# An hourglass-attention and dense kernel rewritten: four-token rows, plane order, key tiles every 112 tokens, PSUM seats given by the plan

## The chip, the cores and the metric

The kernel runs on one core of a Trainium2 chip. The metric is device time in microseconds (us), the median of several executions. A core has TensorE (PE, with its weight loads as PEld), VectorE (DVE), ScalarE (ACT) and GpSimd (POOL); SyncE (SP) issues most transfers, and 16 DMA engines move the data. Matmul results land in PSUM, which has eight banks of 512 float32 columns on 128 partitions; everything else on the chip lies in SBUF.

## The reference

Attention over 8 batches of 8 heads, 576 tokens, 64 features, and then a two-layer dense block on its result:

```python
# q, k, v: (8, 8, 576, 64); factor = 4
q_d, k_d, v_d = means over groups of 4 tokens          # 144 pooled tokens
out_d = softmax(scale * q_d @ k_d.T) @ v_d              # pooled attention
out_up = np.repeat(out_d, 4, axis=2)
mask = np.abs(pos[:, None] - pos[None, :]) < 4          # a band of 7 keys
out_local = softmax(where(mask, scale * q @ k.T, -1e9)) @ v
x = (out_up + out_local), as 4608 tokens x 512
h = x @ w_in                                            # 512 -> 2048
return (h - np.tanh(h)) @ w_out                         # 2048 -> 512, float32
```

## The kernel before

**Work units.** Attention goes by pairs of heads: 32 pairs p, four to a batch. The dense block goes by nine blocks kb of 512 tokens; each has 16 column tiles of `mm1` (four matmuls of 512 columns each, L609) and 16 parts of `mm2` (four each, L636), so there are 1152 dense matmuls. All matmuls are in bf16.

**Order.** Nothing is scheduled by the framework. `Program.op` records each operation with its engine, an estimated duration, keys that it reads and writes, and a priority; `choice` records one that may go to several engines. `order()` is a list scheduler: it plays the engines forward, gives each the ready operation with the lowest priority number, and `emit` writes all instructions in that order of start times. Each engine executes its own in order. Attention has priority 10p, dense matmuls 5000, so dense work fills what attention leaves on PE. Where the plan shows PE idle before the first dense block, `emit` puts filler matmuls (L773).

**One pair.** q and k are loaded as rows of nine tokens (`load_qk`, L291), v as five windows of 128 tokens, one every 120 tokens (`load_v`, L310 to L316). The casts of L408 give `qr`. In the first 16 pairs PE transposes `qr` in nine matmuls (L433) and ACT puts the result in token order in `qk` (L437); from pair 16 on a DMA transpose does it, with two ACT copies (L424). L449 and L454 add four tokens to one for pooled q and k (`half`, `qkd`). Local scores (L468) are ten matmuls of 64 rows, one for each head and query tile of 120 (the last of 96); pooled scores (L484) are four of 144 columns. The two heads use rows 0 to 63 and 64 to 127, and their matmuls run at the same time. ACT takes exponentials (L501, L511, L514), DVE multiplies by the band mask (L504, L517). The outputs (`outs`) are 18 matmuls of 65 columns, nine for each head: five for the local tiles (L528) and four for two blocks of pooled queries (L535), each over two parts of the pooled keys. The 65th column of v gives the sums; L544 takes reciprocals, L546 scales seven blocks into `ln`.

Pooled v comes from PE for pairs below 16 (`pool_v`, six matmuls of 256 columns for two pairs, L381 and L383, in parts of 128 rows), later from a load of four-token rows and two POOL additions (L364, L368), in two parts of 72 rows.

**Back.** In pairs below 16 PE transposes `ln` back: one full matmul (L556), one of 16 rows (L557), five for the local tiles (L560); L587 and L589 add pooled and local result into `xT`. From pair 16 on a DMA transpose and L572, L578 do it.

**PSUM.** Fixed tiles: `ps_ts` and `ps_ox` for attention, two more of each kind for the first batch, whose four banks then become `ps_hy`, four slots that dense work uses in turn.

**Dense order.** Block 0 does all of `mm1` and all of `mm2`; block 1 does `mm1` alone; from block 2 on `mm1` of kb and `mm2` of kb - 1 alternate. The weights are loaded by POOL (L328, L332) as soon as certain v loads are issued.

Of the kernel before, what the change touches and what calls it, by code (L numbers as in the profile page):

```python
# [15 lines left out]
class Program:  # L16
# [6 lines left out]


    LAT = {"PE": 270, "ACT": 150, "DVE": 110, "POOL": 150, "SP": 50, "DMA": 1800}

    def __init__(self):
        self.ops = []
        self.alternatives = {}
        self.touch = []  # L30
        self.fresh = set()
        self.last_write = {}
        self.readers = {}

    def op(self, eng, ns, fn, reads=(), writes=(), pri=0):
        i = len(self.ops)
        deps = set()
        for key in reads:
            if key in self.last_write:
                deps.add(self.last_write[key])  # L40
        for key in writes:
            if key in self.last_write:
                deps.add(self.last_write[key])
            deps.update(self.readers.get(key, ()))
        for key in reads:
            self.readers.setdefault(key, set()).add(i)
        for key in writes:
            self.last_write[key] = i
            self.readers[key] = set()
        deps.discard(i)  # L50
        self.ops.append((eng, ns, fn, deps, pri))
        self.touch.append(set(reads) | set(writes))
        return i

    def choice(self, alternatives, reads=(), writes=(), pri=0):

        i = self.op(None, 0, None, reads, writes, pri)
        self.alternatives[i] = {a[0]: a for a in alternatives}
        return i

    def order(self):
        n = len(self.ops)
        users = [[] for _ in range(n)]
        left = [0] * n
        for i, (_, _, _, deps, _) in enumerate(self.ops):
            left[i] = len(deps)
            for d in deps:
                users[d].append(i)
        at = [0.0] * n
        free, ready, start = {}, {}, [None] * n  # L70

        def make_ready(i):
            for eng in self.alternatives.get(i, (self.ops[i][0],)):
                ready.setdefault(eng, []).append(i)
        for i in range(n):
            if left[i] == 0:
                make_ready(i)
        for _ in range(n):
            best = None
            for eng, cand in ready.items():  # L80
                if not cand:
                    continue
                now = max(free.get(eng, 0.0), min(at[i] for i in cand))
                if eng == "DMA":
                    pick = min((at[i], i) for i in cand)[1]
                else:
                    pick = min((self.ops[i][4], i) for i in cand if at[i] <= now)[1]
                if best is None or now < best[0]:
                    best = (now, eng, pick)
            now, eng, i = best  # L90
            if i in self.alternatives:
                for other in self.alternatives[i]:
                    ready[other].remove(i)
                self.ops[i] = self.alternatives[i][eng] + self.ops[i][3:]
            else:
                ready[eng].remove(i)
            start[i] = now
            end = now + self.ops[i][1]
            free[eng] = end
            for u in users[i]:  # L100
                same = self.ops[u][0] == eng and eng != "DMA"
                at[u] = max(at[u], end if same else end + self.LAT[eng])
# [3 lines left out]
        self.start, self.free = start, free  # L106
        return sorted(range(n), key=lambda i: (start[i], i))

    def idle(self, order, banks, until):

        pe = [i for i in order if self.ops[i][0] == "PE" and self.start[i] < until]
        found = []
        last = 600.0
        for i in pe:
            if self.start[i] - last > 350:
                for name, keys in banks.items():  # L120
                    prev = [e for s0, e, fresh in self.uses[name] if s0 < last]
                    after = [(s0, fresh) for s0, e, fresh in self.uses[name]
                             if s0 >= last]
                    if max(prev, default=0) <= last and (not after or after[0][1]):
                        room = min(self.start[i], after[0][0] if after else until) - last
                        found.append((i, name, room))
                        break
            last = self.start[i] + self.ops[i][1]
        return found

    def emit(self, banks=None, end=None, filler=None):
        order = self.order()
        fill = {}
        if filler:
            until = min(self.start[i] for i in range(len(self.ops)) if end in self.touch[i])
            self.uses = {name: sorted(
                (self.start[i], self.start[i] + self.ops[i][1] + 200, i in self.fresh)
                for i in range(len(self.ops)) if self.touch[i] & set(keys))
                for name, keys in banks.items()}
            for i, name, room in self.idle(order, banks, until):  # L140
                slow = 430 if self.start[i] < 6000 else 230
                fill[i] = (name, int(0.75 * room / slow))
        for i in order:
            if i in fill:
                filler(*fill[i])
            if self.ops[i][2] is not None:
                self.ops[i][2]()
# [3 lines left out]
def kernel(  # L151
# [15 lines left out]
    NHB = NPAIR // 2  # L167
    G = S // 4
    SCALE = 1.0 / float(D) ** 0.5
    A9 = 9  # L170
    G9 = S // A9
    QW = 120
    NT = 5
    NQ = [120, 120, 120, 120, 96]
    KOFF = 585
    N_FF = Dff // 128
    N_DC = Dm // 128
    NBLK = NTOK // 512

# [9 lines left out]
    NQKN, NVST, NVW = 4, 5, 3  # L189
# [3 lines left out]
    mask = fixed("mask", [128, 576], BF16)  # L193
# [3 lines left out]
    qkn = fixed("qkn", [128, 2, A9 * D], FP32, NQKN)  # L197
    vst = fixed("vst", [128, 2, NT, 64], FP32, NVST)
    vw = fixed("vw", [128, 4, NT, 65], BF16, NVW)
    vd = fixed("vd", [128, 2, 4, 65], BF16, NVW)  # L200
    qr = fixed("qr", [128, A9, 128], BF16, 2)
    qk = fixed("qk", [128, 1192], BF16, 2)
    qT = fixed("qT", [128, A9, 128], BF16, 2)
    half = fixed("half", [128, 2, G, 2], FP32)
    qkd = fixed("qkd", [128, 344], BF16, 2)
    v4 = fixed("v4", [72, 2, 2, 4 * D], FP32, 2)
    v2 = fixed("v2", [72, 2, 2, 2 * D], FP32)
    vp = fixed("vp", [72, 2, 2, D + 1], BF16, 2)
    E = fixed("E", [128, 1840], BF16, 2)
    lT = fixed("lT", [128, 7, 128], BF16, 2)  # L210
    warm = lT[0].rearrange("p n c -> p (n c)")[:, 0:512]
    r = fixed("r", [128, 2, 7], FP32, 2)
    ln = fixed("ln", [128, 7, 128], BF16, 2)
    od = fixed("od", [128, G], BF16, 2)
    gT = fixed("gT", [128, N_FF, 512], BF16, 2)
    u = fixed("u", [128, 512], FP32, 3)
    y = fixed("y", [128, Dm], FP32, 3)

    ps_ts = fixed("ps_ts", [128, 2, 512], FP32, pool=psum)
    ps_ox = fixed("ps_ox", [128, 2, 512], FP32, pool=psum)  # L220
    ps_hy = []


    early = ExitStack()
    psum_e = early.enter_context(tc.tile_pool(name="psum_e", bufs=1, space=PSUM))
    ps_ts1 = fixed("ps_ts1", [128, 2, 512], FP32, pool=psum_e)
    ps_ox1 = fixed("ps_ox1", [128, 2, 512], FP32, pool=psum_e)

    def dense_banks():
        early.close()  # L230
        pool = ctx.enter_context(tc.tile_pool(name="psum_d", bufs=1, space=PSUM))
        ps_hy.extend(fixed("ps_hy", [128, 512], FP32, 4, pool=pool))

    P = Program()
    op = P.op
    V, A, T, GP = nc.vector, nc.scalar, nc.tensor, nc.gpsimd


# [7 lines left out]

# [6 lines left out]
    def c_pick():  # L253

        V.memset(pick, 0.0)
        for t in range(4):
            V.tensor_copy(out=pick[:, t, 30 * t:30 * t + 30], in_=group[:, 1:31])
        V.tensor_copy(out=pick[:, 4, 120:128], in_=group[:, 1:9])
        V.tensor_copy(out=pick[:, 5, 112:128], in_=group[:, 9:25])

    def c_mask():

        GP.memset(mask, 1.0)
        m4 = mask[:, 0:480].rearrange("p (t c) -> p t c", c=QW)
        for part, pat in ((m4, [[0, 4], [1, QW]]),
                          (mask[:, 480:576], [[1, 96]])):
            neg = [[-s, n] for s, n in pat]
            GP.affine_select(
                out=part, in_=part, compare_op=ALU.is_ge, fill=0.0,
                base=-1, pattern=neg, channel_multiplier=1)  # L270
            GP.affine_select(
                out=part, in_=part, compare_op=ALU.is_ge, fill=0.0,
                base=7, pattern=pat, channel_multiplier=-1)
        GP.affine_select(
            out=mask[:, 0:QW], in_=mask[:, 0:QW], compare_op=ALU.is_ge,
            fill=0.0, base=-4, pattern=[[0, QW]], channel_multiplier=1)
        GP.affine_select(
            out=mask[:, 480:576], in_=mask[:, 480:576], compare_op=ALU.is_ge,
            fill=0.0, base=99, pattern=[[0, 96]], channel_multiplier=-1)


    def load(ns, fn, keys, cost, pri):
        op("SP", ns, fn, writes=list(keys) + ["queue", ("q", keys[0])], pri=pri)
        op("DMA", cost, None, reads=[("q", keys[0])], writes=keys, pri=pri)

    def load_qk(p):

        b, h0, s = p // NP, 2 * (p % NP), p % NQKN
        for i, src in enumerate((q, k)):
            def issue(i=i, src=src):  # L290
                nc.sync.dma_start(  # L291
# [513 lines left out]
```

## Time and profile before

| | |
|---|---|
| runs | 344.02, 344.06, 345.9 us; median 344.06 |
| profiled execution | span 345.0 us from the first to the last instruction |
| mean granted TensorE clock | 0.980 |
| PE busy | 326.0 us, 94% |
| DVE, ACT, POOL busy | 220.7, 220.5, 152.6 us |
| HBM | 42.46 MB read, 9.44 MB written |
| first dense matmul (L609) | starts at 30.96 us |
| last attention result (L578) | ends at 241.7 us |

Busy time is the union of an engine's instructions. Matmuls overlap in their pipeline, so a dense one lasts 382 ns in the list of groups while the next starts 216 ns after it: the pace is read from one start to the next. In the forms of PE's rows, "72*128" is a matmul of 72 rows and 128 columns of weights, and "72x65" its moving operand. The slices of the page are 8.6 us each, a digit is tenths of busy time.

### The profile page before, as it was taken

What the parts mean: (1) busy time and instruction counts of PE and PEld (TensorE: products, weight loads), DVE (VectorE), ACT (ScalarE), POOL (GpSimd) and SP (SyncE); (2) the same over time, 40 slices, a digit from 0 to 9 for tenths busy, and PEclk for the clock granted to TensorE, in tenths of its full rate; (3) what the DMA queues carried; (4) which work ended last, traced back from release to release, by engine and by line L of the source; (5) the groups of instructions that cost most, each with busy time, mean ns of one, the idle gap of its engine ahead of it and who ended that gap; (6) DMA issues with size and microseconds to landing.
All of it is one profiled execution on the core that took longest, in us unless ns stands there. A gap on an engine that the chain in (4) does not pass through costs nothing.

```text
span 345.0 us, 6688 instructions
## 1 busy us (share of the span) xinstructions
PE 326.0 (94%) x2498; PEld 164.2 (48%) x2498; DVE 220.7 (64%) x365; ACT 220.5 (64%) x353; POOL 152.6 (44%) x196
## 2 busy tenths in 40 slices
PE   4978959999999999999899999999999999999995
PEld 1554435555555554444454444544444444444442
DVE  3687747667999977889789777876333433343300
ACT  3775836658997888979878877974443444344411
POOL 5762224555558747987877688462000000000000
PEclk9599989999999999999999999999999999999999
DMA  7999999779869976999999999723001000100021
GB/s 209 240 230 228 206 301 301 195 227 281 219 149 214 244 203 155 246 232 282 233 210 256 234 251 224 105 67 86 30 30 63 30 30 32 61 30 32 31 91 62
DMA packets 99214, 56.52 MB, mean 164 GB/s; under 512 B 77678, under 2 KB 86382, under 8 KB 99182
## 3 DMA queue, kind: packets, MB, share of 16 engines
q1 hardware_dynamic: 94958, 51.91, 61.2%
q0 software_dynamic: 4224, 4.19, 7.3%
q8 instruction: 19, 0.31, 0.4%
q14 instruction: 13, 0.11, 0.1%
HBM read 42.46 MB, written 9.44 MB: 150 GB/s over the span
## 4 chain that ended last, share of the span: by engine, by line
PE 72%; DMA 11%; DVE 4%; ACT 4%; POOL 3%; issue 3%; SPq 1%; POOLq 0%; ACTq 0%; DVEq 0%
PE ps_hy L636 30%; PE ps_hy L609 29%; DMA qkn<-in_k_dram 9%; PE ps_ts L468 3%; PE ps_ox L528 3%; DMA qkn<-in_q_dram 2%; PE ps_ts L433 2%; ACT qk L424 2%; PE ps_ox L535 2%; DVE E L504 2%; PE ps_ox L560 1%; POOL half L449 1%; DVE gT L620 1%; DVE qr L408 1%; POOL v L364 1%
## 5 line engine op out<-in xcount | busy, mean ns | idle before, releaser
L609 PE MATMUL ps_hy<-xT,w_in_sb 128*128 128x512 bf16 x576 | 146.9, 382 | 1.4 <-DVE xT L589 0.9
L636 PE MATMUL ps_hy<-w_out_sb,gT 128*128 128x512 bf16 x576 | 142.7, 379 | 0.0
L620 DVE TENSOR_TENSOR gT<-ps_hy,u 128x512 bf16<-128x512 f32 x144 | 96.6, 686 | 71.4 <-ACT u L617 70.8
L617 ACT ACTIVATE u<-ps_hy 128x512 f32<-128x512 f32 x144 | 83.9, 598 | 69.3 <-PE ps_hy L609 66.7
L636 PEld LDWEIGHTS <-gT 128*128 128x128 bf16 x576 | 54.6, 98 | 63.2
L609 PEld LDWEIGHTS <-w_in_sb 128*128 128x128 bf16 x576 | 53.0, 98 | 61.1 <-issue 3.6
L449 POOL TENSOR_TENSOR half<-qk 128x576 f32<-128x576 bf16 x29 | 33.4, 1151 | 36.9 <-ACT qk L437 26.0
L424 ACT COPY qk<-qT 128x576 bf16<-128x576 bf16 x32 | 37.8, 1206 | 0.0
L546 DVE TENSOR_TENSOR ln<-ps_ox,r 128x896 bf16<-128x896 f32 x32 | 34.9, 1090 | 1.1 <-DVE r L544 0.2
L501 ACT ACTIVATE E<-ps_ts 128x960 bf16<-128x960 f32 x32 | 31.0, 973 | 6.7 <-PE ps_ts L468 6.4
L504 DVE TENSOR_TENSOR E<-E,mask 128x960 bf16<-128x960 bf16 x32 | 28.4, 889 | 10.0 <-ACT E L501 9.7
L647 ACT COPY y<-ps_hy 128x512 f32<-128x512 f32 x36 | 21.2, 588 | 17.0 <-PE ps_hy L636 16.8
L408 DVE CAST qr<-qkn 128x576 bf16<-128x576 f32 x32 | 23.6, 738 | 8.3 <-DMA qkn<-in_k_dram 8.3
L408 POOL CAST qr<-qkn 128x576 bf16<-128x576 f32 x30 | 21.9, 730 | 15.7 <-DMA qkn<-in_k_dram 9.1
L343 POOL CAST vw<-vst 128x640 bf16<-128x640 f32 x30 | 25.3, 844 | 5.8 <-DMA vst<-in_v_dram 5.8
L437 ACT COPY qk<-ps_ts 128x1152 bf16<-128x1152 bf16 x16 | 18.0, 1125 | 10.8 <-PE ps_ts L433 10.5
L528 PE MATMUL ps_ox<-vw,E 128*128 128x65 bf16 x320 | 21.0, 196 | 2.1 <-DVE E L504 0.9
L454 POOL TENSOR_TENSOR qkd<-half 128x288 bf16<-128x288 f32 x30 | 21.2, 705 | 3.6 <-DVE r L544 2.4
L528 PEld LDWEIGHTS <-E 128*128 128x128 bf16 x320 | 17.0, 99 | 9.3 <-DVE E L517 1.4
L364 POOL TENSOR_TENSOR v<-v 72x512 f32<-72x512 f32 x16 | 20.7, 1296 | 0.6
L468 PEld LDWEIGHTS <-qk 64*128 64x128 bf16 x320 | 9.9, 97 | 17.5 <-issue 15.3
L368 POOL TENSOR_TENSOR vp<-v 72x256 bf16<-72x256 f32 x16 | 11.6, 728 | 14.1 <-PE ps_ox L535 14.0
(71 smaller groups left out, 250.0 us busy)
## 6 DMA issues: line engine op xcount, KB each, us to landing
vst<-in_v_dram SPq DMA_DIRECT2D x62, 160.0 KB, 5.2
qkn<-in_q_dram SPq DMA_DIRECT2D x32, 288.0 KB, 4.3
qkn<-in_k_dram SPq DMA_DIRECT2D x32, 288.0 KB, 4.5
out_dram<-y SPq DMA_DIRECT2D x36, 256.0 KB, 4.1
v<-in_v_dram SPq DMA_DIRECT2D x16, 288.0 KB
w_in_sb<-in_moe_w_in_dram POOLq DMA_DIRECT2D x4, 512.0 KB, 12.4
w_out_sb<-in_moe_w_out_dram POOLq DMA_DIRECT2D x4, 512.0 KB, 20.0
vst<-in_v_dram SPq DMA_DIRECT2D x2, 128.0 KB
```

Source lines behind the costliest of these rows:

```text
L343: P.choice([(eng, ns, lambda fn=fn: fn(out=vw[w][:, 2 * jj:2 * jj + 2, :, 0:64], in_=vst[s])) for eng, ns, fn in CAST_V[p >= NEARLY]], rea ...
L408: P.choice([(eng, ns, lambda dst=dst, srt=srt, fn=fn: fn(out=dst, in_=srt)) for eng, ns, fn in REORDER[p >= NEARLY][h]], reads=[("qkn", sn ...
L424: op("ACT", 600, lambda i=i: A.copy(out=full[:, i].rearrange("p (g a) -> p g a", a=A9), in_=qT[s].rearrange("p a (g i) -> p i g a", i=2)[: ...
L449: eng.tensor_tensor(out=half, in0=four[:, :, :, 0:2], in1=four[:, :, :, 2:4], op=ALU.add)
L501: op("ACT", 870, lambda: A.activation(out=e1, in_=ps[:, :, 0:480], func=AF.Exp, scale=SCALE), reads=ts, writes=[("E", s, 0)], pri=pri)
L504: op("DVE", 700, lambda: V.tensor_tensor(out=e1, in0=e1, in1=mask[:, 0:480].unsqueeze(1).to_broadcast([128, 2, 480]), op=ALU.mult), reads= ...
L528: T.matmul(po[:, hh, 65 * t:65 * t + 65], E[s][:, c:c + 128], vw[w][:, 2 * jj + hh, t, :], start=True, stop=True)
L546: op("DVE", 1010, lambda: V.tensor_tensor(out=ln[s].rearrange("p n (h d) -> p h n d", d=D), in0=blocks[:, :, :, 0:64], in1=r[s].unsqueeze( ...
L609: T.matmul(ps_hy[slot], w_in_sb[:, dc, fc * 128:(fc + 1) * 128], xT[dc][:, kb * 512:kb * 512 + 512], start=(dc == 0), stop=(dc == N_DC - 1))
L617: op("ACT", 490, lambda: A.activation(out=u[us], in_=ps_hy[slot], func=AF.Tanh), reads=[("hy", slot)], writes=[("u", us)], pri=-1)
L620: op("DVE", 620, lambda: V.tensor_tensor(out=gT[g][:, fc, :], in0=ps_hy[slot], in1=u[us], op=ALU.subtract), reads=[("hy", slot), ("u", us) ...
L636: T.matmul(ps_hy[slot], gT[g][:, fc, ts * 128:ts * 128 + 128], w_out_sb[:, fc, :], start=(fc == 0), stop=(fc == N_FF - 1))
```

## The change

The planner becomes `Plan`, and the attention half is written anew. In words:

- q, k (and pooled v from pair 12 on) are loaded as rows of four tokens, on 96 partitions and three slots: four DMAs for q and k where there were two, two for pooled v where there was one.
- The tokens stand in plane order: token 4g + c lies in plane c at place g. q is read from the planes `kq`; k is put in token order in `kt`. `xT` keeps plane order, and the stores to `out` put rows back with a stride of four rows, so a store that crosses a plane is split (64 stores for 36).
- Key tiles start every 112 tokens. Local queries have 120, 112, 112, 112 and 120 columns.
- The outputs are six blocks for seven: the second part of the pooled queries is accumulated into a local block. Pooled keys and v are in two parts of 96 and 48 rows (`ROWS`), 18 matmuls a pair as before.
- Scores are two operations for every pair. q and k are transposed on PE for pairs below 12 (twelve matmuls of 96 rows), by DMA after that; the way back is on PE for all 32 pairs (seven full transposes).
- Pooling of v is by pair, on PE below pair 12. The casts, the pooled additions and the copies may go to more engines. Pairs from 12 on are released by the plan every 7.6 us.
- PSUM is one tile of eight banks; an operation that opens a result names possible seats, and `order()` gives a free one and holds it until the last user. The plan also knows the port that DVE and POOL share, and new durations.
- Dense: block 0 does `mm1` alone, one matmul per operation; then `mm1` of kb and `mm2` of kb - 1 alternate from block 1 on. Openings of dense results are kept in program order by the key "turn".

```diff
-    NQ = [120, 120, 120, 120, 96]
+    STEP = 112
+    G0 = [0, 30, 58, 86, 114]
+    NG = [30, 28, 28, 28, 30]
+    ROWS = [96, 48]
+    NE, NBK = 12, 32
+    PACE, REL = 7600.0, 60000.0
...
+        for n, dst, src, cost in ((0, st[s][:, 0], kv[0:96], 720),
+                                  (1, st[s][0:48, 1], kv[96:144], 360),
+                                  (2, st[s][48:96, 1], qv[0:48], 360),
+                                  (3, st[s][:, 2], qv[48:144], 720)):
+            load(450, lambda dst=dst, src=src: nc.sync.dma_start(out=dst, in_=src),
+                 [("st", s, n)], cost, 10 * p - 3000)
...
+                for c in range(4):
+                    for t in range(3):
+                        o = 288 * (c % 2) + 96 * t
+                        T.transpose(b16[:, c // 2, o:o + 96], qr[s][:, 3 * c + t, :],
+                                    ident[0:96, 0:96])
...
+        op("PE", 240 * cold, score1, reads=[("kt", s), ("kq", s), ("go", "sc", s)],
+           writes=[("scd", p), ("go", "out", s)], pri=pri, opens=(s1, two), slack=slack)
+        op("PE", 200 * cold, score2, reads=[("kt", s), ("kq", s), ("qkd", s)],
+           writes=[("sdd", p), ("go", "out", s)], pri=pri, opens=(s2, two), slack=slack)
...
+            for hh in range(2):
+                def to(n, e, vv, start, stop, kr=128):
+                    T.matmul(po[:, hh, 65 * n:65 * n + 65], E[s][0:kr, hh, e:e + 128],
+                             vv, start=start, stop=stop)
+                for n, t in ((1, 2), (2, 3), (3, 0), (4, 4)):
+                    to(n, E0 + COL[t] - (16 if n < 3 else 0), vw[w][:, hh, t, :], True, True)
+                to(0, 0, vw[w][:, hh, 1, :], True, False)
+                for i in range(2):
+                    to(0, EP + 256 * i + 128, vp[s][0:ROWS[i], hh, i, :], False, i == 1,
+                       ROWS[i])
+                for i in range(2):
+                    to(5, EP + 256 * i, vp[s][0:ROWS[i], hh, i, :], i == 0, i == 1,
+                       ROWS[i])
...
+                for n in range(6):
+                    T.transpose(px[:, 128 * n:128 * n + 128], ln[s][:, n, :], ident)
+                T.transpose(px[:, 768:896], ln[s][:, 0, :], ident)
...
+        step = 1 if kb == 0 else 2
+        for n in range(0, N_DC, step):
+            dcs = range(n, n + step)
+            op("PE", 216 * step, lambda dcs=dcs: mm(dcs),
+               reads=[("w_in", fc // 4)] + [("x", b, j) for b in bs for j in dcs],
+               writes=[("hd", kb, fc)] + (["turn"] if n == 0 else []), pri=5000,
+               opens=(name, seats) if n == 0 else None, uses=[name])
...
         if kb == 0:
             for i in range(16):
                 mm1(kb, i)
-            for i in range(M2_FIRST):
-                mm2(kb, i)
             return
```

## The prediction

> **What bounds the kernel now.** First the page: the share of each engine, then the slices.
>
> ```profile
> span 345.0 us, 6688 instructions
> PE 326.0 (94%) x2498; PEld 164.2 (48%) x2498; DVE 220.7 (64%) x365; ACT 220.5 (64%) x353; POOL 152.6 (44%) x196
> PE   4978959999999999999899999999999999999995
> PEclk9599989999999999999999999999999999999999
> DMA  7999999779869976999999999723001000100021
> ```
>
> TensorE (PE) is full from the seventh slice (52 us) to the end; VectorE (DVE), ScalarE (ACT) and GpSimd (POOL) never are. Between 120 and 240 us, the fullest long stretch in the table by windows, they are busy 96.1, 97.9 and 84.9 of 120 us. So after the start the time is the sum of what PE has to do, and an edit costs what it adds to PE's queue. A busy PE says nothing of its pace, though, so I take the pace from the timeline of PE, from start to start. The first stretch is a late pair's outputs between dense matmuls:
>
> ```profile
> 207.92 1.03 PE L636 MATMUL ps_hy<-w_out_sb,gT 128*128 128x512 bf16 x4
> 208.78 0.32 PE L528 MATMUL ps_ox<-vw,E 128*128 128x65 bf16 x5
> 208.95 0.29 PE L535 MATMUL ps_ox<-vp,E 72*128 72x65 bf16 x4
> 209.07 0.32 PE L528 MATMUL ps_ox<-vw,E 128*128 128x65 bf16 x5
> 209.23 0.29 PE L535 MATMUL ps_ox<-vp,E 72*128 72x65 bf16 x4
> 209.36 1.03 PE L609 MATMUL ps_hy<-xT,w_in_sb 128*128 128x512 bf16 x4
> ```
>
> Four dense matmuls take 0.86 us, 0.216 each; 18 output matmuls take 0.58, 0.032 each, and the 72-row ones (72*128) are as quick as the 128-row ones. The second stretch is of early pairs:
>
> ```profile
> 82.25 0.67 PE L433 MATMUL ps_ts<-ident,qr 128*128 128x128 bf16 x9
> 82.75 1.03 PE L609 MATMUL ps_hy<-xT,w_in_sb 128*128 128x512 bf16 x4
> 83.62 0.22 PE L556 MATMUL ps_ox<-ident,ln 128*128 128x128 bf16 x1
> 83.77 0.18 PE L557 MATMUL ps_ox<-ident,ln 16*128 16x16 bf16 x1
> 83.88 0.43 PE L560 MATMUL ps_ox<-ident,ln 120*128 120x120 bf16 x5
> 84.15 0.60 PE L609 MATMUL ps_hy<-xT,w_in_sb 128*128 128x512 bf16 x2
> 84.67 0.22 PE L468 MATMUL ps_ts<-qk 64*128 64x96 bf16 x2
> 84.73 0.29 PE L484 MATMUL ps_ts<-qkd 64*128 64x144 bf16 x4
> 84.95 1.90 PE L609 MATMUL ps_hy<-xT,w_in_sb 128*128 128x512 bf16 x8
> 86.78 0.39 PE L468 MATMUL ps_ts<-qk 64*128 64x120 bf16 x8
> 87.10 1.04 PE L609 MATMUL ps_hy<-xT,w_in_sb 128*128 128x512 bf16 x4
> ```
>
> The nine transposes of L433 take 0.50 us, 0.056 each. But the one of L556, of the same size, holds the queue 0.15 us before the 16-row one, 0.095 too long. The 16-row one holds it 0.11, against 0.03 for other small ones. Two dense matmuls before a 64-row score take 0.52 instead of 0.43; eight take 1.83 instead of 1.73. Each change between matmuls of many rows (72 to 128) and few (16, 64) thus costs **about 0.095 us**, in either direction.
>
> **PE's bill before.** Dense: 1152 x 0.216 = 248.8. Attention: outputs 32 x 0.58 = 18.6. Scores of the first 16 pairs, in two parts: s2 0.28 and 0.09 to enter, s1 0.32 and 0.10 to enter, 0.79 x 16 = 12.6. Scores of the last 16, in one part (0.49 and 0.10 to enter, timeline at 197.67): 9.4. Transposes of q and k 16 x 0.50 = 8.0; transposes back 16 x 0.53 (83.62 to 84.15) = 8.5; pooling of v 8 x 0.68 (timeline at 87.97) = 5.4. Together 62.5. The end, from PE's last matmul (340.8) to the last store, is 4.2. The rest is 345.0 - 248.8 - 62.5 - 4.2 = **29.5 us**, nearly all before 60 us: no dense matmul starts before 30.96, and then data is late:
>
> ```profile
> POOL half L449 <- ACT qk L437: 10.7, 3, 4.9
> POOL vw L343 <- DMA vst<-in_v_dram: 4.9, 2, 2.6
> POOL qr L408 <- DMA qkn<-in_k_dram: 4.8, 2, 2.5
> ```
>
> These are waits of 30 to 60 us (total, times, longest), while 8 MB of weights and eight pairs share the DMA engines.
>
> **The change on PE, part by part.** *Outputs*: still 18 matmuls of 65 columns a pair, 0.58. But pooled v now lies as 96 and 48 rows, and the order per head is five of 128 rows, then 96, 48, 96, 48. If a 48-row matmul counts as one of few rows, each is entered and left: 4 a pair, 8 changes, 0.76 us, 32 pairs: **24.3 us**. The trace has no 48-row matmul. The bounds are nothing (as for 72 rows) and 0.76 a pair (as for 16 and 64); since 48 lies between two sizes that both pay, I take 0.76.
>
> On this the Trainium skill (TensorEngine Tiling (Array Packing), Key Properties) says that changing the tiling mode drains TensorE, and names modes of 128, 64 and 32 rows. By that 48 rows would need the 64-row mode, and the sum is the one above; by the 72-row row alone it would be 24.3 us less. The page gives no price.
>
> *Scores*: the same columns, now two operations for every pair. The second waits for the pooled q and k (L449 and L454 need 1.9 us on POOL today), so dense matmuls come between and both parts pay entry and exit: 0.80. When both are ready together it is 0.59. I take four of five apart: 0.76 x 32 = 24.3 (18.9 to 25.6). *Transposes of q and k*: twelve of 96 columns on 12 pairs; by columns between 0.052 (120) and 0.03 I take 0.046: 12 x 0.55 = 6.6. *Transposes back*: seven full ones at 0.056 on all 32 pairs, no 16-row one: 0.39 x 32 = 12.5; DMA did this for 16 pairs before. *Pooling of v*: 12 x 6 x 0.056 = 4.0. Outputs 42.9 with their changes. Sum 42.9 + 24.3 + 6.6 + 12.5 + 4.0 = 90.3, **27.8 us more** than 62.5.
>
> **The change elsewhere.** On DVE, ACT and POOL a pair gets about 1 us cheaper: the two ACT copies of L424 (1.2 each) become one to kt (1.25, or 0.8 on DVE, by the plan's own figures), the two mask products (0.89 and 0.42) one, ln has 6 blocks for 7 (1.09 to 0.94), while od (0.28) returns for late pairs and the join reads PSUM (0.75). All of it lies beside PE, whose queue is never empty after 60 us; were that cover gone, it would gain up to 1 us a pair for 24 pairs. The casts have 768 elements a partition for 576, 0.74 to 0.98 if it goes by elements, also covered. DMA: 16 transposes of ln go, 4 of qr and 4 loads of pooled v are added; q and k come as 1 KB rows instead of 2304 bytes. Issues on SP rise: four a pair for q and k (two before), two for pooled v (one), 64 stores for 36. At 0.61 us (L291 in the timeline) the two extra of each of the first four pairs make 4.9 us in SP's queue; v and the next pair's loads stand behind them. At the start the data rate sets the pace, so I count 0 to 3, taken as 1. The last store is still one of 128 rows; the end stays at 4.2.
>
> **The start.** Three effects on the 29.5. (a) Pooling per pair instead of per two, and block 0's first matmuls per head pair, let work begin before the fourth pair: 2 to 5 us gained, taken as 3. (b) Before, block 0's two halves (27.6 us of dense work) needed batch 0 alone. Now the second half stands behind mm1(1, 0) through "turn", which needs pairs 4 and 5: 13.8 us less cover. Pairs 5 and 7 were done at 60.2 and 73.1 (ends of L589); dense work may run dry between about 47 and 60. Taken as 4 lost, 0 to 12. (c) The extra work of the first six to eight pairs, about 0.65 each, falls into waits: 4 gained. With the 1 of SP: 29.5 - 3 + 4 - 4 + 1 = 27.5.
>
> The skill (TensorE: Matmul & The Clock Gate, Why this matters for your kernels) warns that a gap of over about 3 us halves the clock again; here, after the short stalls of 43 to 48 us, the mean granted clock is 0.89 from 45 to 60 us (table by windows), 3.3 us at half, and six dense matmuls from 49.50 on take 2.68 us, 0.45 each. One more such stretch, if (b) makes a long gap, adds 1.7 us.
>
> **Sum**: 248.8 + 90.3 + 4.2 + 27.5 = 370.8 for a span that was 345.0. The runs' median (344.06) lies 0.9 under that span, so the forecast is **370 us**, likeliest 362 to 377.
>
> **Rivals.** *Rows are free*: the 48-row matmuls run like the 72-row ones. Speaks for it: no 48-row row in the trace, and 72 rows pay nothing. The outputs fall to 18.6, attention to 66.0, 3.5 over before; with little extra work to hide, (c) falls to 1, and (b) to 2 since attention is ready sooner; the rest is 28.5, the span 347.5: 346.6 us, 339 to 352, so not slower. The price of a change decides: with 256 of them, under 0.01 us each there is no loss left. Chance 0.17. *Dense work runs dry*: (b) at its upper end and a cold stretch, 10 us more: 380, 376 to 387. For: the late loads above; against: attention still goes first on PE, and the new plan counts 4.0 us of DMA for a pair, nearer to the 230 GB/s of the slices. Chance 0.12. *The new order halves the waits*: the rest falls to 15 since the plan knows ports and seats: 357, 350 to 361. For: 29.5 is there to be had; against: the loads cannot come sooner. Chance 0.09. The forecast keeps 0.62.
>
> A run here tells 1% from none. Of the first rival I put 0.05 to faster, 0.07 to same, 0.05 to slower; 0.04 of the third goes to faster and 0.01 to same, for free rows together with halved waits. That makes faster 0.09, same 0.08, slower 0.83. The range, 344 to 382, holds the forecast, most of the third rival and half of the first and the second.
>
> **What would show it.** Right: in the timeline each 48-row matmul holds PE about 0.13 us and so does the one before it; outputs take 1.3 us a pair; seven back transposes 0.4; score2 apart from score1; DVE, ACT and POOL with waits for PE only. Wrong: 48-row spacing of 0.03, or a PE with gaps after 70 us, which would make another engine or a transfer the bound.

## The result, and the profile after

The changed kernel takes **389.57 us** (median of four runs, 389.07 to 390.91), against 344.13 for the kernel before, run beside it: a ratio of 1.133, interval 1.128 to 1.137. The forecast was 370, the range 344 to 382. The direction was right and the size was not: 45.4 us were lost instead of 26.

The page of the changed kernel, its span, PE's row, PE's slices of 9.7 us and the granted clock:

```profile
span 388.8 us, 7055 instructions
...
PE 356.9 (92%) x2590; PEld 185.8 (48%) x2637; DVE 228.6 (59%) x391; ACT 217.4 (56%) x377; POOL 127.8 (33%) x149
...
PE   5865689879999999999999999999999999999995
...
PEclk9795569996999999999999999999999999999999
```

PE is still full from about 100 us to the end. But its first ten slices are emptier, and in four of them the granted clock is 0.5 to 0.6. So there are two places to look at: what PE does in the full part, and what it waits for in the first 100 us.

**The full part.** A late pair's outputs in the timeline of PE:

```profile
221.27 0.32 PE L539 MATMUL ps<-vw,E 128*128 128x65 bf16 x5
221.43 0.59 PE L539 MATMUL ps<-vp,E 96*128 96x65 bf16 x4
221.95 0.33 PE L539 MATMUL ps<-vw,E 128*128 128x65 bf16 x5
222.12 0.60 PE L539 MATMUL ps<-vp,E 96*128 96x65 bf16 x4
```

Each row of four hides two matmuls of 96 rows and two of 48, in turn. They take 0.52 us of PE (221.43 to 221.95); four of 72 rows took 0.12 before (208.95 to 209.07). From start to start a 96-row matmul ahead of a 48-row one holds PE 0.131 us and the 48-row one holds it 0.133.

**The bill.** One rule for both traces, from each start on PE to the next: a matmul's columns at the full clock, 0.095 us for each change between many rows and few (the number of changes in brackets), and what remains is waiting (unfilled or filled with dummy matmuls, and slow clock). How attention and the waits divide is good to about half a us: by columns alone attention differs by 4.0.

| us | before | after | difference | predicted |
|---|---|---|---|---|
| dense matmuls | 248.8 | 248.8 | 0 | 0 |
| attention without changes of rows | 48.1 | 52.5 | +4.5 | +3.5 |
| changes of rows | 11.5 (124) | 35.2 (372) | +23.7 | +24.3 |
| waits and start | 31.2 | 46.6 | +15.4 | -2 |
| ends of the span | 5.4 | 5.6 | +0.2 | 0 |

The prediction's +24.3 is the outputs alone. Its +3.5 has in it some 19 changes more in the scores and 32 fewer in the transposes; sorted by the rows of this table it says about +4.7 and +23.1. So the terms of attention came out as predicted. The miss is in one row: waits and start.

**The start.** The four pairs of batch 0 are through attention (their x in `xT`) at 23.8, 24.6, 29.7 and 30.9 us before, and at 22.9, 33.9, 42.4 and 50.1 after. Waits of the changed kernel from 20 to 50 us (engine, operation and releaser: total, times, longest):

```profile
POOL vw L351 <- DMA vst<-in_v_dram: 20.7, 1, 20.7
...
ACT vw L351 <- DMA vst<-in_v_dram: 6.8, 1, 6.8
PE ps L382 <- ACT vw L351: 6.7, 1, 6.7
```

And the timeline of ACT, PE and POOL in the same stretch:

```profile
32.41 0.73 ACT L351 CAST vw<-vst 128x640 bf16<-128x640 f32 x1 [6.78 <-DMA vst<-in_v_dram]
33.04 0.27 ACT L588 COPY od<-ps 128x144 bf16<-128x144 bf16 x1
...
25.78 0.68 PE L426 MATMUL ps<-ident,qr 96*128 96x96 bf16 x12
33.18 0.80 PE L382 MATMUL ps<-vw,pick 128*128 128x128 bf16 x6 [6.72 <-ACT vw L351]
...
46.82 0.80 PE L382 MATMUL ps<-vw,pick 128*128 128x128 bf16 x6 [1.61 <-POOL vw L351]
...
48.26 0.84 PE L583 MATMUL ps<-ident,ln 128*128 128x128 bf16 x6
...
46.05 0.72 POOL L351 CAST vw<-vst 128x640 bf16<-128x640 f32 x1 [20.67 <-DMA vst<-in_v_dram]
```

The first line is the cast of v of pair 3 (the fourth). That v was issued at 15.5 and landed at 32.3. ACT stands at it for 6.8 us, and behind it in ACT's order waits the copy `od` of pair 1, whose transposes PE had done by 25.8: pair 1 ends at 33.9 for that reason. PE stands at the pooling of pair 3, ahead of pair 2's second scores. POOL stands 20.7 us at the cast of pair 4's v, which landed at 45.9; PE has that pair's pooling (46.82) ahead of the transposes back of pair 3 (48.26), whose `ln` was ready at 45.5. Every wait is for a load of a later pair, placed ahead of an earlier pair's work. PE's clock follows, in the windows (PE, PEld, DVE, ACT and POOL busy, granted clock, DMA share, GB/s):

```profile
15.00:30.00 15.00, 9.54 (x118) 6.28 (x119) 8.32 (x16) 7.46 (x13) 4.65 (x6) 0.96 1.21 217
30.00:45.00 15.00, 9.82 (x85) 6.34 (x87) 7.67 (x15) 6.21 (x12) 0.00 (x0) 0.50 1.20 218
45.00:60.00 15.00, 12.08 (x87) 6.51 (x87) 7.45 (x14) 7.44 (x14) 3.49 (x4) 0.63 1.07 205
```

The granted clock is half from 28.7, inside the one gap of 6.7 us on PE (26.5 to 33.2), to 56.0.

### The profile page after: what moved, and what is told of

Same layout as the page of the kernel before. It is cut to its first block, busy times and chain, and to the rows that moved or that the text cites. A ratio compares the mean times of both kernels' runs of the same rounds, so it can differ in the third digit from the quotient of the medians.

```text
span 388.8 us, 7055 instructions
## 1 busy us (share of the span) xinstructions
PE 356.9 (92%) x2590; PEld 185.8 (48%) x2637; DVE 228.6 (59%) x391; ACT 217.4 (56%) x377; POOL 127.8 (33%) x149
## 3 DMA queue, kind: packets, MB, share of 16 engines
HBM read 43.65 MB, written 9.44 MB: 137 GB/s over the span
## 4 chain that ended last, share of the span: by engine, by line
PE 77%; DMA 15%; SPq 3%; ACT 2%; issue 2%; POOL 1%; DVE 1%; POOLq 0%; ACTq 0%
PE ps L638 31%; PE ps L614 29%; DMA vst<-in_v_dram 10%; PE ps L539 8%; SPq L311 3%; PE ps L583 3%; DMA st<-in_k_dram 2%; PE ps L485 2%; DMA st<-in_q_dram 2%; PE ps L493 1%; PE ps L499 1%; PE ps L382 1%; PE ps L426 1%; ACT u L625 1%; ACT E L504 0%
## 5 line engine op out<-in xcount | busy, mean ns | idle before, releaser
L614 PE MATMUL ps<-xT,w_in_sb 128*128 128x512 bf16 x547 | 151.5, 389 | 3.8 <-issue 2.3
L628 DVE TENSOR_TENSOR gT<-ps,u 128x512 bf16<-128x512 f32 x144 | 98.5, 688 | 83.8 <-ACT u L625 83.1
L638 PE MATMUL ps<-w_out_sb,gT 128*128 128x512 bf16 x560 | 145.7, 379 | 1.4 <-issue 0.9
L625 ACT ACTIVATE u<-ps 128x512 f32<-128x512 f32 x144 | 85.6, 599 | 70.9 <-PE ps L614 67.1
L539 PEld LDWEIGHTS <-E 128*128 128x128 bf16 (+2 forms) x576 | 35.8, 98 | 19.5 <-DVE E L526 2.9
L539 PE MATMUL ps<-vp,E 96*128 96x65 bf16 (+1 forms) x256 | 38.7, 202 | 0.0
L504 ACT ACTIVATE E<-ps 128x912 bf16<-128x912 f32 x32 | 29.9, 933 | 12.6 <-PE ps L485 11.4
L463 POOL TENSOR_TENSOR half<-kq 128x576 f32<-128x576 bf16 x20 | 26.9, 1346 | 25.8 <-DVE kq L435 23.7
L413 POOL CAST qr<-st 96x768 bf16<-96x768 f32 x32 | 27.8, 882 | 20.7 <-issue 15.6
L651 ACT COPY y<-ps 128x512 f32<-128x512 f32 x36 | 21.1, 586 | 20.7 <-PE ps L638 19.5
L558 DVE TENSOR_TENSOR ln<-ps,r 128x768 bf16<-128x768 f32 x32 | 30.6, 956 | 1.1 <-DVE r L556 0.2
L526 DVE TENSOR_TENSOR E<-E,mask 128x1152 bf16<-128x1152 bf16 x32 | 28.3, 885 | 4.9 <-ACT E L508 4.9
L576 DVE TENSOR_TENSOR xT<-ps,od 128x336 bf16<-128x336 bf16 x64 | 16.3, 298 | 15.5 <-ACT od L588 15.4
```

Source lines behind the costliest of these rows:

```text
L413: (eng, ns, lambda dst=dst, src=src, fn=fn: fn(out=dst, in_=src), port)
L463: eng.tensor_tensor(out=half, in0=flat[:, 0:576], in1=flat[:, 576:1152], op=ALU.add)
L504: A.activation(out=E[s][:, :, E0:E0 + 456], in_=at(s1)[:, :, PS0:512], func=AF.Exp, scale=SCALE)
L526: op("DVE", 760, lambda: V.tensor_tensor(out=el, in0=el, in1=mask.unsqueeze(1).to_broadcast([128, 2, S]), op=ALU.mult), reads=["mask"], wr ...
L539: T.matmul(po[:, hh, 65 * n:65 * n + 65], E[s][0:kr, hh, e:e + 128], vv, start=start, stop=stop)
L558: op("DVE", 960, lambda: V.tensor_tensor(out=ln[s].rearrange("p n (h d) -> p h n d", d=D), in0=blocks()[:, :, :, 0:64], in1=r[s].unsqueeze ...
```

## The experiments

Two theories were to be told apart for each half. For PE's bill: the 48-row matmuls cost a change of rows, or something else does. For the start: (S) loads land later than the plan assumes and engines that keep their order stand at them; against (D) dense work runs dry by its new order, and (P) the engines' work of a pair sets the pace. "After" below is 389.6 us. The kernel before was run beside each experiment, with medians from 343.45 to 346.19, and the ratios are to that; a difference from 389.6 carries this spread, about 1 us, and 2 for h1 and h2.

### Rows of TensorE

**e1_rows96**: the second pooled part as 96 rows.

```diff
-    to(0, EP + 256 * i + 128, vp[s][0:ROWS[i], hh, i, :], False, i == 1, ROWS[i])
+    to(0, EP + 256 * i + 128, vp[s][:, hh, i, :], False, i == 1, 96)
```

> The changed kernel, with the second part of pooled v in the output matmuls taken with 96 rows instead of 48 (rows 48 to 95 of v and of its ones column are zero). The order of all instructions is kept. Theory 'changes of row mode': the 256 changes between 96 or 128 rows and 48 go, each about 0.10 us by the trace after (a 48-row matmul holds PE 0.133 us, the one before it 0.13, against 0.03), less what lies in waits before 60 us: 389.6 falls by 22 to 25, to about 366. Rival 'the small matmuls are slow for another reason (the vp operand, accumulation in a shared block)': 387 to 390.

Measured 367.51, ratio 1.068 (1.062 to 1.074): 22.1 us less. Changes of rows fall from 372 to 124 (35.2 to 11.6 us); the waits stay (47.2). A pair's four pooled matmuls are back at 0.12 us:

```profile
207.73 0.32 PE L539 MATMUL ps<-vw,E 128*128 128x65 bf16 x5
207.88 0.29 PE L539 MATMUL ps<-vp,E 96*128 96x65 bf16 x4
```

**e5_before_48rows**: the reverse, in the kernel before.

```diff
-    E[s][0:vv.shape[0], c + G * i:c + G * i + 128], vv, ...
+    E[s][0:(48 if new and i else vv.shape[0]), ...], vv[0:48] if new and i else vv, ...
```

> The kernel before, where the second part of the pooled keys of pairs 16 to 31 is taken with 48 rows instead of 72 in the output matmuls (24 of 144 pooled keys are left out there). Nothing else changes. Theory 'changes of row mode': 16 pairs x 8 changes x 0.10 us = 12.8 more, 355 to 358, since PE is full in that stretch. Rival 'what e1 gained came from the changed kernel's own order': 343 to 346.

Measured 355.41, ratio 1.034 (1.029 to 1.039): 12.0 us more for 128 further changes, 0.094 each. Nothing else was touched; 24 of 144 pooled keys are left out there. The price of the change of rows is shown in both directions.

**e6_before_full_back**: the kernel before, with its 16-row transpose back made a full one, so that these pairs need no change of rows on the way back.

```diff
-            T.transpose(px[1][:, 128:144], ln[s][0:16, 6, :], ident[0:16, 0:16])
+            T.transpose(px[1][:, 128:256], ln[s][:, 6, :], ident)
```

> The kernel before, where the 16-row transpose back of pairs 0 to 15 takes all 128 rows of its block, so that no change of row mode is left on the way back. By the trace before, L556 then holds PE 0.056 us instead of 0.15 and the second one 0.056 instead of 0.11: 0.15 a pair, of which the pairs after the start (10 to 12) count: 1.5 to 2 us less, about 342. Rival 'the transposes wait for something else there': 343.5 to 344.5.

Measured **341.94**, ratio 0.995 (0.992 to 0.998): faster than the kernel before by 1.5 us, a small gain but clear of the noise. Both transposes now take 0.056 us, where they held PE 0.15 and 0.11:

```profile
88.09 0.22 PE L556 MATMUL ps_ox<-ident,ln 128*128 128x128 bf16 x1
88.14 0.22 PE L557 MATMUL ps_ox<-ident,ln 128*128 128x128 bf16 x1
```

### The start: dense order, and the number of issues

**e3_mm2first**: the changed kernel with the dense order of before (block 0's `mm1` and `mm2`, then `mm1` of block 1).

```diff
         if kb == 0:
...
+            for i in range(16):
+                mm2(kb, i)
             return
+        if kb == 1:
+            for i in range(16):
+                mm1(kb, i)
+            return
```

> The changed kernel with the dense order of the kernel before: all of mm2 of block 0 straight after its mm1, block 1 with mm1 alone, so the plan makes a new order. Theory 'late data': block 0 starts as late as now (first stretch of ten or more dense matmuls at 51 us) and the total falls by at most 4: 385 to 391. Rival 'dense work runs dry between blocks 0 and 1': the waits of 60 to 100 us (about 8 us by the spacing) go, total 378 to 383.

Measured 389.51, ratio 1.132 (1.125 to 1.139): no change; batch 0 ends at 49.0. (D) falls.

**e4_split_before**: the kernel before, with four loads for a pair's q and k where it had two.

```diff
-                nc.sync.dma_start(out=qkn[s][i::2], in_=src[b, h0:h0 + 2]...)
+                for e in range(2):
+                    nc.sync.dma_start(out=qkn[s][i::2, e], in_=src[b, h0 + e]...)
```

> The kernel before with each load of q and of k split by head, four issues a pair instead of two; the bytes, row sizes and order are kept. Theory 'more issues on SP let the weights overtake': v of pair 3 is issued near 17 us instead of 11, behind the w_in quarters that POOL issues at 12.8 to 15.2; batch 0 ends 4 to 10 us later than 30.9 and the total rises to 347 to 354. Rival 'the number of issues does not matter, since the data rate sets the start': 343 to 346.

Measured 356.55, ratio 1.034 (1.025 to 1.043): **12.8 us more** for the same bytes. Batch 0 ends at 43.7 instead of 30.9, 12.8 later. The v of pair 2 is issued at 13.7 and 14.3, behind the first two loads of w_in, and ACT stands at its cast for 8.6 us. The v of pair 3 is issued at 14.9 and 15.6, behind three of the four loads of w_in (13.1 to 14.7); with two loads it went out at 10.8 and 11.4, ahead of them all (12.8 on). The waits of 15 to 45 us are of the kind seen after:

```profile
PE ps_ts L469 <- ACT qk L438: 8.8, 1, 8.8
ACT vw L344 <- DMA vst<-in_v_dram: 8.6, 1, 8.6
```

So two further issues for each pair can cost this kernel some 13 us by themselves.

### The start: weights ahead of v

**e2_hold**: in the changed kernel POOL reads a column of the landed v before it issues a weight, so that the weights can't overtake it.

```diff
         def issue():
+            if (name, f) != ("w_in", 0):
+                GP.tensor_copy(out=held, in_=vst[after[1]][:, :, 0, 0])
```

> The changed kernel, where POOL reads one column of v of pair 3 before it issues the second to fourth quarter of w_in, and of v of pairs 4 to 7 before each quarter of w_out, so that these weights start only when that v has landed. The order of all other instructions is kept. Theory 'weights overtake q, k, v at the start': v of pair 3 lands near 20 us instead of 32, v of pair 4 near 27 instead of 46, the last result of batch 0 near 36 instead of 50, and the total falls by 10 to 18, to about 375. Rival 'SP's six issues for a pair set the pace': the loads land as late as now, total 386 to 392.

Measured 398.86, ratio 1.158 (1.151 to 1.165): 9 us *more*. The v of pairs 3 and 4 land at 23.5 and 27 to 28 as wanted, but POOL's own queue stands at the held weights, and pair 1's additions behind them start at 42.1:

```profile
POOL held L338 <- DMA vst<-in_v_dram: 26.1, 4, 11.5
```

A late load was traded for a late engine.

**e8_plan_hold**: the same, with the plan told of the wait, so that it orders POOL around it.

```diff
-        op("POOL", 1000, issue, reads=[("q", after)],
+        op("POOL", 1000, issue, reads=[("q", after)] if first
+           else [("vst", after[1], 0), ("vst", after[1], 1)],
```

> As e2 (three quarters of w_in start when v of pair 3 has landed, the quarters of w_out when v of pairs 4 to 7 has), but the plan knows of the wait, so that it places POOL's other work around it; in e2 the additions of q and k stood behind the held weights until 42 us. The order of all engines is made anew. Theory 'weights overtake q, k, v': v of pair 3 lands near 23, batch 0 ends 6 to 12 us before 50.1, total 376 to 384. Rival 'the loads of the first four pairs and the order of PE set it, not the weights': 387 to 395.

Measured 382.43, ratio 1.113 (1.108 to 1.117): 7.1 us less. The number is in the range expected, its path is not: the pairs end at 22.2, 26.0, 31.9 and 49.7, so the first three are near the kernel before, but batch 0 ends only 0.4 us sooner; batch 1 ends 10.6 us sooner (79.3 for 89.9). The fourth is held by one queue again, in the waits of 30 to 52 us (line numbers are 7 higher here):

```profile
ACT vw L358 <- DMA vst<-in_v_dram: 12.6, 3, 6.9
...
PE ps L546 <- ACT E L511: 6.9, 1, 6.9
```

ACT stands at the cast of pair 5's v, landed at 39.0; behind it is what pair 3's outputs need.

**f3_plan_hold_late**: e8 with the plan's allowance for a transfer raised.

```diff
-    LAT = {"PE": 270, "ACT": 160, "DVE": 130, "POOL": 160, "SP": 50, "DMA": 1900}
+    LAT = {"PE": 270, "ACT": 160, "DVE": 130, "POOL": 160, "SP": 50, "DMA": 5000}
```

> The kernel of e8_plan_hold (382.4 us), with the planner's allowance for a transfer raised from 1900 to 5000 ns, so that it places casts and poolings that wait for a landing further back in the engines' orders. Theory (an engine's order has a later pair's cast ahead of an earlier pair's work): the fourth pair of batch 0, which ended at 49.7 because ACT stood at a cast of pair 5, ends at about 40, and the time falls by 5 to 9 us, to 373 to 377. Rival (the transfers' rate alone): the order changes nothing, 381 to 384.

Measured 388.6, ratio 1.132 (1.128 to 1.137): 6 us worse than e8, a miss. Batch 0 ends at 48.5. ACT still stands at pair 5's cast at 39.1: that v took 13.5 us from issue to landing (25.5 to 39.0), so an allowance of 5 us was still too early there; the other orders changed with it.

**f1_one_quarter** and **f2_before_one_quarter**: three quarters of the weights' traffic taken out of the changed kernel and of the kernel before. (That is 6.3 MB of reads from HBM, 43.65 to 37.36, and not the 1.5 MB of the expectation.)

```diff
         def issue():
+            if f:
+                return
...
-                T.matmul(..., w_in_sb[:, dc, fc * 128:(fc + 1) * 128], ...
+                T.matmul(..., w_in_sb[:, dc, fc % 4 * 128:(fc % 4 + 1) * 128], ...
```

> The changed kernel, of whose two weight matrices only the first quarter is loaded, and every matmul of the dense layers uses that quarter: 1.5 of 2 MB of transfers leave the first 50 us, the instructions of the five engines and their plan stay as they are. Theory (the start: transfers of later pairs' v land late behind the weights, and engines that take their work in order stand at them): batch 0 ends at about 35 us instead of 50.1, and the time falls by 10 to 15 us, to 375 to 380. Rival (the new order of work on the engines costs the start by itself, whatever the transfers do): batch 0 ends at 45 us or later and the time is 385 or more.

> The kernel before with the same cut: only the first quarter of both weight matrices is loaded and used. It is the control of the run above. Theory: here the weights were issued behind the v of batch 0 and stand little in its way, so batch 0 ends at 28 to 31 us (30.9 before) and the time falls by 0 to 4 us, to 340 to 344. Rival: the weights cost this kernel's start as much as the changed one's, 10 us or more, and then what they do is no account of the difference between the two.

Measured 379.92, ratio 1.109 (1.103 to 1.114), and 340.78, ratio 0.993 (0.991 to 0.995). The changed kernel gains 9.6 us and the kernel before 2.7; batch 0 ends at 39.3 and at 30.5. So the weights weigh more on the changed start, by 6 to 7 us, not quite half of the 15.4 that the waits grew by. But 39.3 is still 8.8 later than 30.5, with q and k of pair 3 landing at 22.0: the weights are not all of it. The chain of work that ended last in f1 says where the rest lies, in that run (start, us, what; line numbers are 2 higher here):

```profile
8.07 3.97 DMA st<-in_q_dram
12.04 1.21 DVE qr L415
...
27.74 0.76 DVE half L465
28.50 0.68 DVE E L528
29.18 0.05 issue
29.23 1.47 PE ps L541 x18
...
37.67 0.64 PE ps L585 x6
```

From 12.0 us to the end of batch 0 it holds no transfer: PE, DVE and ACT release one another. By this chain, with most of the weights out of the way, the engines' own work (theory P) or its order in the plan holds the changed start.

### The start: who issues what, and when

**e7_v_on_act**: ACT's queue issues batch 0's v, where its order has them.

```diff
-                nc.sync.dma_start(out=vst[s][:, i], ...
+                (nc.scalar if p < NP else nc.sync).dma_start(out=vst[s][:, i], ...
```

> The changed kernel, where v of the first four pairs is issued by ACT's queue instead of SP's; order and bytes are kept. Theory 'SP's queue lets the weights overtake': SP has 16 issues instead of 24 before pair 4, v of pair 3 is issued before 13 us and lands before 22 instead of at 32, batch 0 ends 6 to 12 us earlier than 50.1 and the total falls by as much, to 378 to 384. Rival 'the order on PE and POOL at the start is slow whatever the loads do': 387 to 392.

Measured 389.52, ratio 1.133 (1.128 to 1.138). The premise failed: ACT issued the v of pair 3 only at 17.5 and 19.2 us, later than SP does. The loads of SP and ACT take eight semaphores in turn, and an issue waits until the load that had its semaphore before has landed: these two followed landings at 17.43 and 19.18. So the run says nothing of the number of issues.

**g1_load_order**, **g2_before_order** and **g3_order_one_quarter**: the change also moved v of a pair ahead of q and k of the next; g1 takes that back, g2 does it in the kernel before.

```diff
-                 [("st", s, n)], cost, 10 * p - 3000)
+                 [("st", s, n)], cost, 10 * p - 3000 - (12 if p < NP else 0))
```

> The changed kernel with the order of the kernel before for the loads of batch 0: q and k of the next pair ahead of v of this one (q0, q1, v0, q2, v1, q3, v2, v3 instead of q0, v0, q1, v1, q2, v2, q3, v3). Theory (the changed order of the loads makes q and k of the fourth pair land late, at about 21 us): they land 2 to 4 us sooner and the time falls by 3 to 8 us from 389.5. Rival (the number of issues and the weights alone): the sum of the bytes ahead of the weights is the same, within 2 us of 389.5.

> The kernel before with the changed kernel's order of the loads of batch 0: v of a pair ahead of q and k of the next. Theory: the fourth pair's q and k land 2 to 3 us later and the time rises by 2 to 6 us, to 346 to 350. Rival: no difference, 343 to 345.

> f1_one_quarter (one quarter of the weights loaded and used, 379.9 us) with the load order of the kernel before. If weights and order are both causes and add up, batch 0 ends at 34 to 36 us instead of 39.3 and the time is 373 to 377; if the order counts for nothing, 379 to 381.

g1: 390.27, ratio 1.134 (1.130 to 1.138), no change. g2: 350.57, ratio 1.019 (1.016 to 1.022), 6.3 us more, and batch 0 ends at 34.8. g3: 381.58, ratio 1.109 (1.107 to 1.112), as f1. The order of loads alone can cost the kernel before 6 us; its first load of w_in then goes out at 9.2 instead of 12.8, ahead of pair 3's k and v. Yet putting it back gives the changed kernel nothing: v of pair 2 now lands at 28.5 instead of 18.9, and the queues stand at that.

**h1_v_at_head_of_act**: all of batch 0's v at the head of ACT's queue, where nothing waits ahead, and w_in behind the last q.

```diff
+            if p < NP:
+                op("ACT", 600, issue, writes=[("vst", s, i), ("q", ("vst", s, i))], pri=-9990)
...
-        load_w(moe_w_in, w_in_sb, "w_in", f, ("vst", (2 + f) % NVST if f < 2 else 3, 1))
+        load_w(moe_w_in, w_in_sb, "w_in", f, ("st", 3, 3))
```

> The changed kernel with the eight loads of batch 0's v at the head of ACT's queue, where nothing waits before them, so that SP has only the sixteen of q and k of these pairs; the four loads of w_in wait for the last of these sixteen issues, and the plan takes POOL's cast of a v before a load of w_out. No byte and no arithmetic is taken away. Theory (SP's list of 24 issues for batch 0 and the weights that overtake it make the start long): all of q, k and v of batch 0 is issued by 10 us and lands by 20, batch 0 ends at 31 to 36 us instead of 50.1, and the time falls by 13 to 18 us, to 371 to 377. Rival (the five engines' work of a pair sets the pace of the start, each pair some 6 to 9 us): batch 0 ends at 42 us or later, and the time is 383 or more.

Measured 395.09, ratio 1.143 (1.134 to 1.153): no gain, and at most a small loss, since the interval overlaps that of the changed kernel. Two lines of the timeline (POOL, then PE) and one of ACT's waits say why:

```profile
38.24 0.82 POOL L420 CAST qr<-st 96x768 bf16<-96x768 f32 x1 [7.36 <-DMA st<-in_q_dram]
...
39.17 1.12 PE L433 MATMUL ps<-ident,qr 96*128 96x96 bf16 x12 [3.54 <-POOL qr L420]
```

```profile
ACT L358 <- DMA st<-in_k_dram: 10.9, 1, 10.9
```

ACT does no work of its own until 10.9 us: the eight issues took until then, 4.5 us for themselves and the rest in waits for landings, as in e7 (the last two, at 8.15 and 10.47, followed landings at 8.13 and 10.46). w_in was behind q in the plan only, since no data passes between the two: it went out from 7.5 on. The q of pair 3 waited in the same way (issued at 18.06, after a v of ACT's that landed at 18.05; the last part went out at 18.4 and landed at 25.0). Then the outputs of pairs 2 and 3 were done by 36, but their transposes back stand on PE behind those of *pair 4's* q and k (39.17), whose q landed at 38.1. Batch 0 ends at 45.3.

### Both together

**f4_rows_plan_hold_late**: f3 and e1 in one kernel.

> The run above with the second part of the pooled v as 96 rows with zeros, as in e1_rows96. If the two causes are apart and add up, it is 22 us below the run above, 351 to 355; if a part of the 22 us was idle time of the start that rows had a share in, it lies 5 us or more above that.

**g5_order_hold_rows**: e8, g1 and e1 in one.

> The changed kernel with three undone parts together: the load order of g1, the weights held behind v of batch 0 with the plan knowing it (e8_plan_hold, -7), and the 96 rows of e1_rows96 (-22). If they add up: 389.5 - 22 - 7 - 5 = 355, and so still above the kernel before. If the start is recovered in whole: 349.

**h2_v_at_head_rows**: h1 and e1 in one.

> The run above with the 96 rows of e1_rows96. If the two causes add up, it is 22 us below the run above, 349 to 355, and what then stays over the kernel before is the two or three us of attention's bill that are no row changes, and 4 us of later waits. If the start costs nothing more with the weights in their place, it is below 349.

f4: 365.69, ratio 1.066 (1.060 to 1.072), 22.9 below f3. g5: 362.15, ratio 1.052 (1.050 to 1.055), 20.3 below e8 (its load order, g1's, was not run with e8 alone). h2: 374.52, ratio 1.084 (1.077 to 1.092), 20.6 below h1. The rows are worth 20 to 23 us whatever the start does: the two causes are apart and add up, to 2 or 3 us. The totals all lie above what was expected, since the start was not recovered. The best version of the changed kernel found, g5, is still 18 us behind the kernel before.

## Why the prediction was right or wrong

**PE's bill was right.** The largest unknown, the price of a 48-row matmul, was taken at 0.76 us a pair; e1 gave back 22.1 us of the 24.3 and e5 cost 12.0 of the 12.2 that half of the pairs should. The rule of the Trainium skill that was weighed there (TensorEngine Tiling (Array Packing), Key Properties) decided rightly over the 72-row row. Without changes of rows attention came to +4.5 for about +4.7. "Rows are free" is refuted.

**The start was wrong, and with it the sum.** The step that failed is "At the start the data rate sets the pace, so I count 0 to 3, taken as 1", together with (a), "2 to 5 us gained, taken as 3". Waits and start were to shrink by 2 us and grew by 15.4, from 31.2 to 46.6. The rate is indeed much the same (218 GB/s from 15 to 45 us, 221 before). What changed is *whose* bytes move. SP needs more issues for a pair, POOL issues the weights on its own, and all four loads of w_in (8.7 to 14.6) are out ahead of v of pair 3 (15.0); before, they stood behind it. I had that in hand (4.9 us of issues, "v and the next pair's loads stand behind them") and wrote it off against the rate. The delay doesn't stay with its transfer either: engines keep the plan's order, so one late v stops work of earlier pairs on ACT, PE and POOL, and PE's clock halves. Batch 0 ends 19.2 us later and the waits grow by 15.4; in e4 it is 12.8 for 12.8. The end of batch 0 is no exact measure, though: e8 gained 7.1 us with batch 0 at 49.7, as late as in the changed kernel. As for (a), dense work does begin sooner, at 24.10 us instead of 30.96, but only ten dense matmuls of the trace start before 50 us, where the kernel before has 54. A sign of being wrong that the prediction named is there: PE has gaps after 70 us (its slices from 68 to 87 us are 0.8 and 0.7).

**"Dense work runs dry"** is nearest in number (380) and wrong in kind: e3 put the order back and nothing moved. (b), taken as 4, was nothing. (c) was not measured by itself.

**"The new order halves the waits"** went the other way; f3 shows how sensitive that order is, 6 us for one number of the plan.

**What stays open.** The weights account for 6 to 7 us of the start (f1 against f2). That more issues alone can cost 13 is shown in the kernel before, but not by taking them away in the changed one, since its rows need the four loads; the two overlap and don't add. Of the 39.1 us between f1 and f2, PE's bill makes 28.2 (4.5 and 23.7), so some 11 us of waits remain with most of the weights gone, and up to the end of batch 0 f1's chain lies on the engines' work and order alone. Which of the two, (P) or the plan's order, isn't settled, nor how the loss divides in the changed kernel itself: no version put batch 0's loads as early as before with all bytes kept.

## What to carry to other kernels

A matmul of few rows between matmuls of many costs about 0.19 us, going in and coming out: pad it with zeros to the neighbours' rows when the data is there anyway. When loads are split, write down what each queue issues before the last load of the first work unit, other queues' bulk transfers included, and compare landing times, not the total rate. A static order made from assumed landings turns one late transfer into a stop of every engine that has its consumer ahead of older work.

## What the runs showed of the hardware

- A 48-row matmul followed at once by a 64-row score is only 0.007 us ahead of it: between 48 and 64 rows there is no change to pay, while 96, 72 and 128 rows go together.
- An issue itself can become slow: two loads of v took SP 6.19 us from 24.73 on (0.45 and 5.69), where one took 0.39 to 0.53 in the first 6 us. The DMA engines moved 217 GB/s around then; no run shows that this is the reason.
- After one gap of 6.7 us on PE the clock stayed at half for 27.3 us, through matmuls with short gaps. That such a gap halves it agrees with the page on the clock gate cited in the prediction. A long gap isn't needed, though: in f1 the clock is at half from 33.0 to 43.3 us, with no gap of PE over 1.4 us in the 9 us before (it was busy 2.04 of the last 3.40). What kept it at half for 27.3 us no run tells.
